# Attention loads: queries and keys sent without the pace of the other loads and ahead of value halves, a wider pace, weights a slot later

## The chip, the cores and the metric

The kernel runs on one core of one Trainium2 chip. The metric is the device time of one execution in microseconds, lower is better.

## The reference

An attention with global and local tokens is followed by two feed-forward layers. Batch is 4, there are 8 heads of 64, 512 local and 32 global tokens.

```python
k_all = np.concatenate([k_g, k_l], axis=2)
v_all = np.concatenate([v_g, v_l], axis=2)
out_g = np.matmul(sm(scale * np.matmul(q_g, k_all.transpose(0, 1, 3, 2))), v_all)
s_ll = scale * np.matmul(q_l, k_l.transpose(0, 1, 3, 2))
s_ll = np.where(np.abs(pos[:, None] - pos[None, :]) <= 32, s_ll, -1e9)
s_lg = scale * np.matmul(q_l, k_g.transpose(0, 1, 3, 2))
out_l = np.matmul(sm(np.concatenate([s_lg, s_ll], axis=-1)), v_all)
x = np.concatenate([out_g, out_l], axis=2)      # 4 x 8 x 544 x 64 -> 2176 x 512
h = x @ w_in                                    # 512 x 2048
x = np.where(h > 0, h, np.exp(np.minimum(h, 0)) - 1) @ w_out
h = x @ w2_in                                   # the second layer
x = np.where(h >= 1, h, np.where(h <= -1, 0, (h + 1) ** 2 / 4)) @ w2_out
```

## The kernel before, in words

The program has two stages. In the first, the planned stage, every instruction of every engine is pinned to the order in which it is written (`eng = pinned`; its records all carry line 113, the line of the helper `Pinned`). In the second (`eng = free`, from line 756 on) a scheduler orders the instructions of the two feed-forward layers.

The planned stage works through 24 units: for each batch and each two pairs of heads a local unit of the first pair, a global unit of both pairs, and a local unit of the second pair. Three units in turn, with two pairs of heads, are called a period here. A unit has parts (`scores`, `top`, `expo`, `turn`, `copy`, `values`, `norm`, `back`, `high`, `low`), and the loop over `n` at line 726 runs the scores of unit `n`, the values of unit `n - 1` and the end of unit `n - 2` in one slot, with pieces of the first layer's weights (`early_weights`) and of its first matmuls (`early_ups`) between. At the end of a slot `arrive(n)` issues loads. `r = n % 3` is the slot within a period: 0 for the slot of the first local unit, 1 for that of the global unit, 2 for that of the second local unit.

All loads of this stage go out on SyncE's queue, in order. They are:

- the queries `q_sb` (544 words of 4 bytes on each of 128 partitions) and the keys `k_sb` (576 words) of a pair of heads, by `load_qk`, two buffers each. The buffer of the keys comes free when the global unit's scores (`sg`) or the second local unit's (`s`) have read it. Before a pair's local scores GpSimd spreads its keys inside the buffer (`spread_keys`), and before the global scores it copies the global queries to `diag` (`spread_queries`);
- the values `v_sb` of a pair in two halves (1040 words each), by `load_v`, six buffers. `V_UNTIL` and the formula beside it in `arrive` say how many halves have been sent by the end of slot `n`;
- six pieces of the first layer's weights, `wraw` (1024 words each, one buffer): `next(next(sent, ...))` sends one at `r == 2`, that is in slots 2, 5, 8, 11, 14 and 17. `early_weights` takes the pieces up from slot 4 on, three slots for each: in slots 4, 7, 10 and so on ScalarE (`top`, line 180) and VectorE (`rest`, line 181) read the raw words for the first time, in the next slot VectorE for the last time.

`load` sets a pace: from the seventh load on, each load waits until the loads sent before it, counted back from itself, are landed as far as they don't fit into `IN_FLIGHT` words per partition together with it (2700 words are 1.38 MB). The wait is SyncE's, and all later loads stand behind it.

Order of the loads over one period, from slot `r = 2` on, before: (q k w v) (v v) (q k v). The brackets are slots.

Of the kernel before, what the change touches and what calls it, by code (L numbers as in the profile page):

```python
# [51 lines left out]

UP_STEP = 4

V_UNTIL = {0: 2, 1: 4, 2: 6, 3: 8, 4: 9, 5: 11}

LAG = 3

W_SHARE = 0.7

IN_FLIGHT = 2700
FIRST_LOADS = 6
WARM_UP = 10

# [2 lines left out]
def band_attention_then_two_mlps(  # L67
# [55 lines left out]

    loads = []

    def load(out, src, words):

        ins = eng.sync.dma_start(out, src)
        if eng is not pinned:
            return  # L130
        flying, older = words, len(loads)
        while older and flying + loads[older - 1][1] <= IN_FLIGHT:
            older -= 1
            flying += loads[older][1]
        if older and len(loads) >= FIRST_LOADS:
            tc.add_manual_dep(
                ins.ins, loads[older - 1][0].ins.name, LANDED, reason="loads in flight"
            )
        loads.append((ins, words))
# [22 lines left out]
    def prep(wraw_p, wtmp_p, layer, f, c0, n, raw_tag="wraw"):  # L162
# [7 lines left out]
        hi, lo = (w[:, c0:c0 + n] for w in wtiles[layer, f])  # L170
        raw = wraw_p.tile([P, n], U64, tag=raw_tag, name="wraw")
        load(raw, (w1, w2)[layer][f][:, c0:c0 + n], 2 * n)
        words = raw.bitcast(U32).rearrange("p (n two) -> p n two", two=2)
        low, high = words[:, :, 0], words[:, :, 1]
# [202 lines left out]
    with ExitStack() as actx:  # L377
# [30 lines left out]
        def load_qk(b, hp):  # L408
            q_sb = raw_p.tile([P, S], F32, tag="q", name="q_sb")
            k_sb = raw_p.tile([P, KPAD + NSUB * 64], F32, tag="k", name="k_sb")  # L410
            both = [(q_sb, qT), (k_sb[:, 0:KPAD], kT)]
            for sb, dram in both if b + hp else both[::-1]:
                load(sb, dram[b, hp], sb.shape[1])
            loaded[b, hp] = [q_sb, k_sb, diag[(NPAIR * b + hp) % 4]]

        def load_v(b, hp, es=(0, 1)):
            for e in es:
                v_sb = win_p.tile([P, half, 2, VW], F32, tag="v", name="v_sb", bufs=6)
                load(v_sb, vwin[b, hp, :, half * e:half * e + half], half * 2 * VW)
                landed.setdefault((b, hp), []).append(v_sb)  # L420

        def spread_keys(b, hp):

            k_sb = loaded[b, hp][1]
            right = k_sb[:, KPAD:].rearrange("p (a c) -> p a c", a=NSUB)
            after = k_sb[:, SG + 32:KPAD].rearrange("p (a c) -> p a c", a=NSUB)
            glob = k_sb[:, 0:SG].rearrange("p (o c) -> p o c", o=1)
            if b + hp == 0:
                eng.vector.tensor_copy(right[:, :, 0:32], after)
                eng.scalar.activation(  # L430
                    right[:, :, 32:64], glob.to_broadcast([P, NSUB, SG]), AF.Copy
                )
                return
            eng.gpsimd.tensor_scalar(right[:, :, 0:32], after, 1.0, 1.0, ALU.mult, ALU.mult)
            eng.gpsimd.tensor_scalar(
                right[:, :, 32:64], glob.to_broadcast([P, NSUB, SG]), 1.0, 1.0, ALU.mult, ALU.mult
            )

        def spread_queries(b, hp):

            for c in (hp - 1, hp):
                if hp % 2:
                    q_sb, dq = loaded[b, c][0], loaded[b, c][2]
                    for h in range(2):
                        r = 64 * h
                        eng.gpsimd.tensor_scalar(
                            dq[r:r + 64, 32 * h:32 * h + 32], q_sb[r:r + 64, 0:32], 1.0, 1.0,
                            ALU.mult, ALU.mult,
                        )
# [194 lines left out]
        pairs = [(b, hp) for b in range(B) for hp in range(NPAIR)]  # L644
# [8 lines left out]
        for _ in range(WARM_UP):  # L653
            eng.tensor.matmul(idle, zeros[:, 0:P], zeros)
        load_qk(*pairs[0])
        eng.scalar.dma_start(mask_sb, mask)
        eng.scalar.dma_start(eye_sb, eye)
        load_qk(*pairs[1])
        load_v(*pairs[0])
        for t in diag:  # L660
# [45 lines left out]
        def arrive(n):  # L706

            g, r = divmod(n, 3)
            p = 2 * g + 1
            if r == 1 and p + 1 < len(pairs):  # L710
                load_qk(*pairs[p + 1])
            elif r == 2 and p + 2 < len(pairs):
                load_qk(*pairs[p + 2])
                next(next(sent, iter([0])))
            while ahead and len(ahead) > 2 * len(pairs) - V_UNTIL.get(n, 4 * g + 5 + r):
                load_v(*ahead.pop(0))
            if r == 0 and g and p < len(pairs):
                spread_queries(*pairs[p])
            elif r == 1 and p < len(pairs):
                spread_keys(*pairs[p])  # L720
            elif r == 2 and p + 1 < len(pairs):
                spread_keys(*pairs[p + 1])

        ahead = [(*pair, (e,)) for pair in pairs[1:] for e in range(2)]
        live, first = {}, {}
        for n in range(len(units) + 2):
            if n > UP_AT:
                next(ups, None)
            part(n, "scores")
            part(n - 2, "norm")  # L730
            part(n - 1, "turn")
            part(n - 1, "copy")
            part(n - 2, "back")
            part(n - 2, "high")
            part(n, "top")
            part(n - 2, "low")
            part(n, "expo")
            if n >= PREP_AT:
                next(weights, None)
            if n >= UP_AT:  # L740
                next(ups, None)
            part(n - 1, "values")

            arrive(n)
            if n == len(units):

                s_ctx.close()
                ps_dn.append(mpool("ps_dn0", 1, space=PSUM))
                for f in chunks[0][1]:
                    down(0, chunks[0][1], 0, f, made[0, f, 0], first, range(KT // 2))  # L750
# [139 lines left out]
```

## Time and profile before

| | |
|---|---|
| median of 3 runs | 871.85 us (870.28 to 872.03) |
| profiled execution | 869.4 us, span of its instructions 867.6 us |
| granted TensorE clock, mean | 0.994 of full |
| matrix multiplies, busy | 847.8 us, 98% of the span |
| VectorE, ScalarE, GpSimd busy | 584.1, 431.6, 27.8 us |
| DMA | 65.43 MB, 75 GB/s over the span |

PE is TensorE's matrix multiply, PEld its weight load, DVE VectorE, ACT ScalarE, POOL GpSimd, SP SyncE, and a q behind an engine's name its queue (an instruction that is issued, not executed). Times of rows are counted from the start of the span. The time between an engine's instructions is called idle, and a releaser is what ended it as far as semaphores show. "issue" is time in which the engine waited for nothing that the profile shows. The planned stage ends near 138 us.

### The profile page before, as it was taken

How to read it: one execution, taken by the hardware profiler on the slowest of the kernel's cores; microseconds unless marked ns; L12 is line 12 of the kernel's file. 1: busy time of each engine (PE TensorE's matmuls, PEld its weight loads, DVE VectorE, ACT ScalarE, POOL GpSimd, SP SyncE). 2: the span in 40 equal slices, each digit the busy share in tenths (PEclk: the TensorE clock that was granted, in tenths of full speed). 3: DMA queues.
4: the chain of work that ended last, by engine and by line, in shares of the span. 5: the costliest groups of instructions: out<-in, count | busy, mean ns of one | idle time of the engine just before them, and what ended most of it. 6: DMA issues, size and time to landing. Idle time of an engine off the chain costs nothing.

```text
span 867.6 us, 14526 instructions
## 1 busy us (share of the span) xinstructions
PE 847.8 (98%) x5946; PEld 696.9 (80%) x5946; DVE 584.1 (67%) x1130; ACT 431.6 (50%) x755; POOL 27.8 (3%) x66
## 2 busy tenths in 40 slices
PE   8888999999999999999999999999999999999998
PEld 5666778888888888888888888888888888888886
DVE  4688884878536873834389897368859754845455
ACT  5666874666335543533257564456335333433332
POOL 2113110000000000000000000000000000000000
PEclk9899999999999999999999999999999999999999
DMA  7777742321200220100012112002201200000014
GB/s 261 246 241 256 231 148 87 108 99 65 81 1 7 94 94 1 59 39 1 1 49 97 49 50 97 0 9 98 89 1 49 97 1 1 0 1 1 2 59 147
DMA packets 19027, 65.43 MB, mean 75 GB/s; under 512 B 3984, under 2 KB 4240, under 8 KB 15248
## 3 DMA queue, kind: packets, MB, share of 16 engines
q1 hardware_dynamic: 18672, 64.23, 21.7%
q8 instruction: 47, 0.77, 0.4%
q10 hardware_dynamic: 288, 0.26, 0.1%
q14 instruction: 20, 0.16, 0.1%
HBM read 60.03 MB, written 4.46 MB: 74 GB/s over the span
## 4 chain that ended last, share of the span: by engine, by line
PE 91%; DMA 7%; POOL 1%; ACT 0%; issue 0%; SPq 0%; DVE 0%; POOLq 0%
PE dn L320 40%; PE up L247 39%; DMA k_sb<-in_kT 3%; DMA v_sb<-in_vwin 3%; PE up L244 3%; PE dn L337 3%; PE pt L113 1%; PE s L113 1%; PE up L113 1%; PE po L113 1%; DMA wraw<-in_w 1%; POOL k_sb L113 1%; PE sg L113 1%; PE dn L113 0%; PE tg L113 0%; PE up L273 0%
## 5 line engine op out<-in xcount | busy, mean ns | idle before, releaser
L320 PE MATMUL dn<-gh,wh 128*128 128x512 f32 x506 | 196.9, 389 | 0.0
L320 PE MATMUL dn<-gl,wh 128*128 128x512 f32 x506 | 196.8, 389 | 0.0
L320 PE MATMUL dn<-gh,wl 128*128 128x512 f32 x506 | 196.3, 390 | 0.0
L247 PE MATMUL up<-xh,wl 128*128 128x512 f32 x492 | 192.5, 391 | 0.0
L247 PE MATMUL up<-xh,wh 128*128 128x512 f32 x492 | 191.6, 389 | 0.0
L247 PE MATMUL up<-xl,wh 128*128 128x512 f32 x492 | 191.6, 389 | 0.0
L278 ACT ACTIVATE gh<-g 128x512 fp32r<-128x512 f32 x123 | 77.8, 632 | 119.2 <-DVE g L267 71.9
L297 DVE TENSOR_TENSOR acc<-dn,acc 128x512 f32<-128x512 f32 x128 | 84.9, 686 | 48.5 <-PE dn L320 48.4
L282 DVE TENSOR_TENSOR gl<-g,gh 128x512 fp32r<-128x512 f32 x123 | 84.7, 689 | 39.2 <-ACT gh L278 38.1
L320 PEld LDWEIGHTS dn<-gl,wh 128*128 128x128 f32 x506 | 95.0, 188 | 19.8
L320 PEld LDWEIGHTS dn<-gh,wh 128*128 128x128 f32 x506 | 95.0, 188 | 19.5
L320 PEld LDWEIGHTS dn<-gh,wl 128*128 128x128 f32 x506 | 95.0, 188 | 19.4
L247 PEld LDWEIGHTS up<-xh,wh 128*128 128x128 f32 x492 | 92.4, 188 | 19.3
L247 PEld LDWEIGHTS up<-xl,wh 128*128 128x128 f32 x492 | 92.4, 188 | 18.9
L247 PEld LDWEIGHTS up<-xh,wl 128*128 128x128 f32 x492 | 92.4, 188 | 18.7
L258 ACT ACTIVATE g<-up,half_sb 128x512 f32<-128x512 f32 (+1 forms) x69 | 47.0, 681 | 113.6 <-PE up L247 104.9
L266 DVE SCALAR_TENSOR_TENSOR g<-g 128x512 f32<-128x512 f32 (+1 forms) x69 | 47.0, 681 | 59.4 <-ACT g L258 59.3
L264 DVE SCALAR_TENSOR_TENSOR g<-up,g 128x512 f32<-128x512 f32 x64 | 43.5, 679 | 62.4 <-ACT g L255 62.3
L253 ACT ACTIVATE g<-up 128x512 f32<-128x512 f32 x64 | 37.8, 591 | 87.0 <-PE up L247 81.8
L267 DVE TENSOR_TENSOR g<-g,e 128x512 f32<-128x512 f32 (+1 forms) x69 | 47.0, 681 | 3.6
L180 ACT ACTIVATE top<-wraw 128x1024 f32<-128x1024 f32 x29 | 33.6, 1157 | 28.4 <-DMA wraw<-in_w 23.3
L255 ACT ACTIVATE g<-g,one_sb 128x512 f32<-128x512 f32 x64 | 45.9, 717 | 1.8
(112 smaller groups left out, 931.5 us busy)
## 6 DMA issues: line engine op xcount, KB each, us to landing
wraw<-in_w SPq DMA_DIRECT2D x29, 1024.0 KB, 4.8
v_sb<-in_vwin SPq DMA_DIRECT2D x32, 520.0 KB, 4.8
k_sb<-in_kT SPq DMA_DIRECT2D x16, 288.0 KB, 3.9
q_sb<-in_qT SPq DMA_DIRECT2D x16, 272.0 KB, 4.4
outT<-acc SPq DMA_DIRECT2D x16, 256.0 KB, 2.1
wraw<-in_w SPq DMA_DIRECT2D x6, 512.0 KB, 4.3
outT<-acc_rows SPq DMA_DIRECT2D x4, 64.0 KB, 2.2
mask_sb<-in_mask ACTq DMA_DIRECT2D x1, 192.0 KB, 3.5
```

The costliest lines, as they stand in the source:

```text
L113: return lambda *args, **kw: tc.keep_in_program_order(fn(*args, **kw))
L247: eng.tensor.matmul(self.ps, w, x, start=k == 0, stop=k == 3 * KT - 1)
L253: eng.scalar.activation(self.g, self.ps, AF.Exp)
L255: eng.scalar.activation(self.g, self.g, AF.Relu, bias=one_sb, scale=-1.0)
L258: eng.scalar.activation(self.g, self.ps, AF.Relu, bias=half_sb, scale=0.5)
L264: eng.vector.scalar_tensor_tensor(g, self.ps, 0.0, g, ALU.max, ALU.subtract)
L266: eng.vector.scalar_tensor_tensor(g, g, 1.0, g, ALU.min, ALU.mult)
L267: eng.vector.tensor_tensor(g, g, self.e, ALU.add)
L278: eng.scalar.activation(self.gh, self.g, AF.Copy)
L282: eng.vector.tensor_tensor(self.gl, self.g, self.gh.bitcast(F32), ALU.subtract)
L297: eng.vector.tensor_tensor(a, ps, a, ALU.add)
L320: eng.tensor.matmul(banks[d], w[:, d * P:(d + 1) * P], g, start=f == fs[0] and k == 0, stop=f == fs[-1] and k == 2,)
```

## The change

`load` gets a parameter `paced`; queries and keys are sent with `paced=False`, so that they wait for no other load (they still wait for their own buffers, and later loads still count them). `IN_FLIGHT` goes from 2700 to 3200 words (1.64 MB). A piece of weights is sent at `r == 0`, from the second period on, in place of `r == 2`: in slots 3, 6, 9 and so on. In the slots `r == 0` one half of values less is sent, and in the slots `r == 1` one more, behind the queries and keys of that slot. The order over a period becomes (q k v) (w v) (q k v v).

```diff
-V_UNTIL = {0: 2, 1: 4, 2: 6, 3: 8, 4: 9, 5: 11}
+V_UNTIL = {0: 2, 1: 4, 2: 6, 3: 7, 4: 9, 5: 11}
...
-IN_FLIGHT = 2700
+IN_FLIGHT = 3200
...
-    def load(out, src, words):
+    def load(out, src, words, paced=True):
...
-        if older and len(loads) >= FIRST_LOADS:
+        if paced and older and len(loads) >= FIRST_LOADS:
...
-                load(sb, dram[b, hp], sb.shape[1])
+                load(sb, dram[b, hp], sb.shape[1], paced=False)
...
                 load_qk(*pairs[p + 2])
+            elif r == 0 and g:
                 next(next(sent, iter([0])))
-            while ahead and len(ahead) > 2 * len(pairs) - V_UNTIL.get(n, 4 * g + 5 + r):
+            while ahead and len(ahead) > 2 * len(pairs) - V_UNTIL.get(n, 4 * g + (4, 6, 7)[r]):
                 load_v(*ahead.pop(0))
```

## Rows read from the trace of the kernel before

**Rows 1.** The page: TensorE's busy time; instruction queue (packets, MB, DMA share).

```profile
PE 847.8 (98%) x5946; PEld 696.9 (80%) x5946; DVE 584.1 (67%) x1130; ACT 431.6 (50%) x755; POOL 27.8 (3%) x66
...
q8 instruction: 47, 0.77, 0.4%
```

**Rows 2.** Stretches: length, PE, PEld, DVE, ACT, POOL busy, clock, DMA share, GB/s.

```profile
138.40:867.60 729.20, 725.51 (x3243) 602.01 (x3240) 484.89 (x692) 337.41 (x509) 0.00 (x0) 1.00 0.14 49
...
2.00:8.00 6.00, 4.48 (x74) 2.09 (x74) 2.04 (x14) 1.69 (x6) 1.25 (x5) 1.00 1.00 342
2.00:112.85 110.85, 96.93 (x2253) 75.11 (x2253) 82.60 (x367) 76.86 (x204) 23.58 (x54) 0.95 0.78 251
...
51.04:67.47 16.43, 14.32 (x339) 11.35 (x339) 13.99 (x57) 11.80 (x31) 4.25 (x9) 1.00 0.76 242
```

**Rows 3.** TensorE's waits, 24 to 138 us: in total, times, longest.

```profile
PE s L113 <- POOL k_sb L113: 7.0, 5, 2.1
PE s L113 <- issue: 1.9, 2, 1.8
PE po L113 <- DMA v_sb<-in_vwin: 1.3, 1, 1.3
PE pog L113 <- DMA v_sb<-in_vwin: 0.9, 1, 0.9
PE tg L113 <- DVE og L113: 0.3, 1, 0.3
```

**Rows 4.** The chain that ended last, one period: start, us, what.

```profile
56.90 3.60 DMA v_sb<-in_vwin
...
60.57 5.07 DMA k_sb<-in_kT
...
65.78 1.64 POOL k_sb L113 x2
```

**Rows 5.** SyncE's waits, 9 to 121 us: in total, times, longest.

```profile
SPq L113 <- DMA v_sb<-in_vwin: 42.2, 25, 3.3
```

**Rows 6.** The page's DMA issues: KB each, median us to landing.

```profile
v_sb<-in_vwin SPq DMA_DIRECT2D x32, 520.0 KB, 4.8
k_sb<-in_kT SPq DMA_DIRECT2D x16, 288.0 KB, 3.9
q_sb<-in_qT SPq DMA_DIRECT2D x16, 272.0 KB, 4.4
...
wraw<-in_w SPq DMA_DIRECT2D x6, 512.0 KB, 4.3
```

**Rows 7.** TensorE's timeline: start, us, instruction, idle before and releaser.

```profile
31.00 1.03 PE L113 MATMUL pog<-v_sb,pgT 64*64 64x130 f32 x10 [0.91 <-DMA v_sb<-in_vwin]
33.74 1.96 PE L113 MATMUL s<-k_sb,q_sb 64*32 64x128 f32 x64 [1.71 <-POOL k_sb L113]
...
55.60 1.22 PE L113 MATMUL sg<-k_sb,diag 128*64 128x272 f32 x12
...
67.47 1.16 PE L113 MATMUL s<-k_sb,q_sb 64*32 64x128 f32 x64 [2.08 <-POOL k_sb L113]
...
82.99 1.83 PE L113 MATMUL s<-k_sb,q_sb 64*32 64x128 f32 x64 [1.20 <-POOL k_sb L113]
```

**Rows 8.** SyncE's timeline: issues of one period.

```profile
52.34 0.33 SPq L113 DMA_DIRECT2D wraw<-in_w  x1
...
60.57 0.33 SPq L113 DMA_DIRECT2D k_sb<-in_kT  x1
```

**Rows 9.** Stretches as in rows 2, where the granted clock is low.

```profile
32.00:38.85 6.85, 5.14 (x114) 4.28 (x116) 2.86 (x21) 1.81 (x6) 3.21 (x8) 0.50 0.83 273
83.20:86.63 3.43, 3.43 (x72) 2.73 (x56) 3.16 (x21) 1.23 (x2) 2.18 (x6) 0.50 0.65 204
```

**Rows 10.** The weights' load of 52.34: flight; ScalarE's timeline: its first reader.

```profile
DMA to landing us min/median/max: 4.5/4.5/4.5
...
59.63 0.70 ACT L113 ACTIVATE top<-wraw 128x512 f32<-128x512 f32 x1
```

## The prediction

> **What bounds the kernel now.** I read the page first: TensorE is busy 847.8 of 867.6 us [rows 1], so at most 19.8 us of the span are to be had without removing matmuls. The windows by stage then say where these lie. From 138.4 us to the end, TensorE is busy 725.51 of 729.20 us [rows 2]; the edit touches only the planned stage before that, and a shift there moves the end by the same amount. Third, the waits of TensorE between 24 and 138 us [rows 3]: 7.0 us in five waits of the score matmuls `s` for the keys that GpSimd spreads, 1.3 and 0.9 us in one wait each for value halves, 1.9 us in the sequencer's own time ("issue"), 0.3 us for VectorE. Fourth, the chain that ended last, in one period of the stage (three units, two head pairs) [rows 4]: the end of the global scores is followed by a value half in flight for 3.60 us, then the keys in flight for 5.07 us, then GpSimd for 1.64 us, and only then the scores. The keys are not sent when their buffer is free but when a value half has landed. SyncE's own waits say the same in total: 42.2 us, 25 times, for value halves [rows 5]. The pace, not the buffers, orders this stage.
>
> The bytes of a period follow from the issues of the page [rows 6]: four value halves, two pairs of queries and keys, one piece of weights, 4 x 520 + 2 x 560 + 512 = 3712 KB, 3.80 MB. The stage moves 251 GB/s on the mean and 342 GB/s between 2 and 8 us, when the first loads are out together at a DMA share of 1.00 [rows 2]. At 251 a period takes 15.1 us, at 342 it takes 11.1. TensorE alone: from the end of `sg` (55.60 + 1.22 = 56.82) to the start of `s` at 67.47 are 10.65 us, 2.08 of them waiting [rows 7]; the window from `s` to `s` is 16.43 us long with 14.32 busy [rows 2]. So TensorE needs about 14.5 us, or 262 GB/s. Loads and TensorE are close, and a rate 5% above the present one makes TensorE the limit.
>
> **The change part by part.** *Queries and keys without the pace.* No instruction is added; two waits of SyncE per pair go. The keys' own buffer still makes them wait for the global scores. In the period shown the scores end at 56.82 and the keys go at 60.57 [rows 7, 8]: 3.75 us that the pace cost.
>
> *One value half goes behind instead of ahead.* The order on SyncE's queue was (q k w v)(v v)(q k v); it becomes (q k v)(w v)(q k v v). Counted along the queue, the period's first keys lose one 520 KB half ahead of them, 2.1 us at 251 GB/s or 1.6 at 342. The moved half now stands behind one query and one key load (560 KB, 2.3 us at 251); it is needed only a period later, so this costs nothing except at the start (below). With both parts the keys can go right behind the global scores, and must be spread 8.6 us later (10.65 less 2.08): 5.07 us in flight and 1.64 on GpSimd [rows 4] need 6.7. I take all four later waits as gone: 7.0 less the first, 1.71 [rows 7], is **5.3 us**. Bounds: 2.1 us for all of them together, if the loads stay the limit at 251 GB/s, since one half fewer ahead is then gained once and not per period; 5.3 at best.
>
> *The start.* The first three waits, 1.3 + 0.9 + 1.7 = 3.9 us, lie between 24 and 34 us. Two halves of values gain a 512 KB piece of weights that no longer stands ahead of them, so the 1.3 us goes. But the second half of the fourth pair now lands behind the fifth pair's queries and keys. Up to it there are 5 x 560 + 512 + 8 x 520 KB and 256 KB of constants, 7728 KB or 7.91 MB. From 2 us on that is 33.5 us at 251 GB/s, 25.1 at 342; at 280 it is 30.3. The value matmuls of the global rows would want it at 31.00 - 0.91 - 1.3 = 28.8 [rows 7]. At 280 they wait 1.5 us, and 2.4 of the 3.9 are won; the bounds are a loss of about 0.8 (matmuls end near 34.5 where `s` now starts at 33.74) and a gain of 3.9. I take **2.4**, with 280 as the rate, for the reason of the next paragraph.
>
> *3200 in place of 2700 words under way.* 18.5% more bytes in flight. If the rate went with them it would be 251 x 1.185 = 297 GB/s; half of that effect gives 274; the stretch without a pace shows 342. 280 is between, and above the 262 that TensorE needs. Bounds 251 and 342.
>
> *The clock.* In two stretches the granted clock is 0.50, the lower of its two levels (1.2 GHz): 6.85 us with 5.14 busy, and 3.43 us, all busy [rows 9]. The first begins as the wait of 1.71 us starts (33.74 - 1.71 = 32.03), the second 0.2 us after the wait that ends at 82.99 [rows 7]: both go with a wait for keys. The score matmuls take 1.96 us there and 1.16 elsewhere [rows 7], so 0.41 of the busy time is the price: 0.41 x 8.57 = 3.5 us. Fewer waits should take the second stretch (1.4) and, since a wait stays at the start, half of the first (1.05): **2.5**. Bounds 0 and 3.5.
>
> *What is late next.* Where no keys are waited for, the 0.3 us for VectorE shows [rows 3]; in the four periods freed I charge 0.3 each, **-1.2** (bounds 0 and, with VectorE busy 13.99 of 16.43 us [rows 2], some 2).
>
> *Code.* Two "issue" waits of together 1.9 us [rows 3] stand in the scores; with the value wait ahead of another run of scores gone, one more can show there: **-1.0**, bounds 0 and -1.8. The page has 47 instruction packets of 0.77 MB in all [rows 1], which more data under way could also delay. The Trainium skill (Runtime: NRT & Kernel Launch, section Instruction fetch mechanics) says that a sequencer fetches its next 16 KiB block through a DMA queue of its own while it executes, and that the cost is mostly hidden; the size agrees (0.77 MB / 47), the "issue" rows do not quite. By that page this term would be 0 and the sum 1.0 us better.
>
> *Weights a slot later.* A piece of weights went at 52.34, landed 4.5 us later at 56.84, and its first reader ran at 59.63 [rows 8, 10]: 2.8 us to spare. In the queue it now stands behind one more half, 2.1 us. It still fits, so I charge nothing; ScalarE, which would stand in `top` with the copies `pT` for TensorE queued behind it, is the cover that would be gone if it came later (rival 3). The wait of the weights for their own buffer (VectorE's reads) gets shorter by the slot.
>
> Sum: -5.3 - 2.4 - 2.5 + 1.2 + 1.0 = **-8.0 us**. The profiled execution took 869.4, so 861.4; the runs shown have a median 2.45 us above it (871.85), so I predict **863.9**.
>
> **The rivals.** *1. The wait only moves into the queue.* Keys sent earlier stand behind the same bytes, and the rate stays near 251. For it: the DMA share is already 0.78 over the stage [rows 2], and a landing takes 5.07 us for 288 KB, so loads do queue. Against it: the rate is 342 where nothing paces. It gives the one half, 2.1 us, and perhaps the 1.4 us of the second slow stretch less what the start loses (0.8): 869.7 down to 868, taken as 869. The Trainium skill (DMA: Bandwidth & Descriptors, section Queues, rings and completion order) has the rule behind this: SyncE's loads share one ring on each DMA engine, and descriptors are consumed in ring order, so an unpaced load does not overtake.
>
> *2. No change.* The keys might be held by their buffer and not by the pace, or a wait of VectorE or ScalarE takes the place of each one removed. For it: VectorE is busy 85% of the window. Against: the 3.75 us between the end of `sg` and the keys, and a value landing between the two in the chain. 871.85, within 0.2%.
>
> *3. Slower: the weights come late.* If the piece really goes a whole slot later, with the half of 4.6 us after it (56.90 [rows 4] less 52.34), and lands another 2.1 behind it, it is 6.7 us later, 3.9 past its reader; so five pieces with as little to spare cost at most 19.5 us, and nothing if the others have 6.7 to spare. Taken at 11, a little over the middle, less the 8.0 won, this is +3: 874.9. It decides from a cost of 1.9 us a piece on (8.0 + 1.7 over five), a delay of 4.7; one half is 2.1.
>
> **How the numbers follow.** 0.2% is 1.7 us, about what a measurement of this kernel can tell from no change. Forecast (gain of 5 to 12 us, 860 to 867): 0.60. Rival 1 (867 to 870): 0.22. Rival 2: 0.10. Rival 3: 0.08. The best case is 7.0 + 2.2 + 3.5 = 12.7 us with nothing given back, 859.1; I give less than 0.04 to anything under 860. The range 860 to 871 leaves out that, rival 3 and most of rival 2. Faster by over 0.2%: the forecast and nearly all of rival 1, 0.81; same 0.11; slower 0.08.
>
> **What would show it.** Right: the waits of `s` for GpSimd's keys fall from 7.0 to under 1.5 us; keys go within 1 us of the end of `sg`; periods of about 14.5 us; the stage's rate at 265 GB/s or more; matmuls of the free stage begin near 130 instead of 138.4; a wait of 1 to 2 us for values near 29 us. Rival 1: the keys' flight grows from 4 to 6 us or more, and they land when they did. Rival 3: ScalarE waits for `wraw` in `top`. The prediction is wrong if the rate does not rise above 262, if a value or weight wait larger than 2 us takes the place of the key waits, or if the clock falls in more places than two.

## The result and the profile after

The changed kernel takes 863.83 us (median of 4 runs, 860.65 to 864.34) against 871.94 us (870.28 to 874.63): ratio 0.9896, 95% interval 0.9862 to 0.9931, that is 6.0 to 12.0 us less. Its profiled execution took 864.34 us with a span of 862.6, so the two profiled executions are 5.1 us apart and the medians 8.1. The traces below account for the 5.1; the rest lies in the other runs, of which more further down.

Where the time went is read from the first matmul of the down products in TensorE's timeline, before and after (start, us, instruction):

```profile
134.03 0.50 PE L113 MATMUL dn<-gh,wl 128*128 128x512 f32 x1
```

```profile
128.95 0.50 PE L113 MATMUL dn<-gh,wl 128*128 128x512 f32 x1
```

From there to the end are 867.6 - 134.03 = 733.6 us before and 862.6 - 128.95 = 733.65 after. The whole difference lies in the planned stage, as forecast. TensorE's waits in that stage after the change, against [rows 3] (in total, times, longest):

```profile
PE po L113 <- issue: 2.6, 2, 1.8
PE s L113 <- issue: 1.8, 1, 1.8
PE tg L113 <- DVE og L113: 1.0, 3, 0.3
PE ot L113 <- DVE o_sb L113: 0.2, 1, 0.2
```

No wait for keys is left (7.0 us before) and none for values (2.2). What is left are waits of the sequencer's own, 4.4 us against 1.9, and VectorE's, 1.2 against 0.3. The periods of the stage and its rate, to be held against [rows 2] (length, PE, PEld, DVE, ACT, POOL busy, clock, DMA share, GB/s):

```profile
2.00:105.00 103.00, 94.47 (x2234) 73.03 (x2233) 79.45 (x363) 75.57 (x201) 25.29 (x58) 0.98 0.84 275
...
46.06:60.34 14.28, 14.25 (x341) 11.35 (x339) 12.02 (x55) 11.84 (x33) 3.90 (x8) 1.00 0.83 262
60.34:75.04 14.70, 14.34 (x341) 11.36 (x339) 13.09 (x56) 12.33 (x34) 3.60 (x9) 1.00 0.79 260
75.04:89.76 14.72, 14.35 (x340) 11.38 (x339) 13.10 (x56) 12.33 (x34) 3.69 (x9) 1.00 0.78 261
```

From one run of scores to the next a period is 14.3 to 14.7 us with 14.3 busy: TensorE is the limit, at some 260 GB/s. The DMA share does not tell this: it was 0.76 to 0.78 before as well [rows 2], when TensorE waited for loads. SyncE's waits, against the 42.2 us of [rows 5]:

```profile
SPq L113 <- PE s L113: 21.7, 7, 5.8
SPq L113 <- PE pt L113: 16.5, 9, 3.9
SPq L113 <- DMA v_sb<-in_vwin: 11.4, 12, 2.0
```

Loads are now held back mostly by TensorE, whose reads make the buffers free, and much less by loads under way: SyncE's waits for landings of all kinds come to 17.9 us in that stretch, 66.5 before. The period of [rows 8], in SyncE's timeline after:

```profile
47.45 0.33 SPq L113 DMA_DIRECT2D wraw<-in_w  x1
47.88 0.37 SPq L113 DMA_DIRECT2D v_sb<-in_vwin  x1
48.36 0.87 SPq L113 DMA_DIRECT2D q_sb<-in_qT  x1
51.81 0.33 SPq L113 DMA_DIRECT2D k_sb<-in_kT  x1
53.66 1.68 SPq L113 DMA_DIRECT2D v_sb<-in_vwin  x2
```

The global scores of that period run from 50.61 for 1.22 us, to 51.83: the keys go as they end, where they went 3.75 us later before.

TensorE's clock, however, was no better in this execution. The stretches at the lower level, against [rows 9] (same columns as the periods):

```profile
35.74:39.16 3.42, 3.42 (x21) 2.57 (x20) 2.15 (x6) 0.36 (x2) 0.00 (x0) 0.50 0.93 309
104.01:110.84 6.83, 6.83 (x98) 5.11 (x97) 4.84 (x23) 4.43 (x12) 2.07 (x4) 0.50 0.63 185
```

Together 10.25 us, as long as before (10.28), and all of it busy where before 8.57 was. Each starts within a microsecond after one of the sequencer's waits, which in the timeline are these (the third wait ends at 103.16):

```profile
25.42 0.43 PE L113 MATMUL po<-v_sb,pT 128*32 128x65 f32 x16 [0.89 <-issue]
35.60 0.34 PE L113 MATMUL po<-v_sb,pT 128*32 128x65 f32 x3 [1.76 <-issue]
103.16 0.42 PE L113 MATMUL s<-k_sb,q_sb 64*32 64x128 f32 x8 [1.81 <-issue]
```

### The profile page after: what moved, and what is told of

It is laid out like the page before. It is cut to its first block, busy times and chain, and to the rows that moved or that the text cites. A ratio compares the mean times of both kernels' runs of the same rounds, so it can differ in the third digit from the quotient of the medians.

```text
span 862.6 us, 14522 instructions
## 1 busy us (share of the span) xinstructions
PE 849.1 (98%) x5946; PEld 697.5 (81%) x5946; DVE 580.8 (67%) x1130; ACT 431.6 (50%) x755; POOL 27.6 (3%) x66
## 4 chain that ended last, share of the span: by engine, by line
PE 96%; DVE 2%; issue 1%; ACT 1%
PE dn L320 40%; PE up L247 39%; PE up L244 3%; PE dn L337 3%; PE po L113 2%; PE s L113 2%; PE up L113 2%; PE pt L113 2%; PE pog L113 1%; PE sg L113 1%; PE tg L113 1%; PE ot L113 1%; DVE top L113 1%; PE dn L113 1%; PE idle L113 0%
```

## The experiments

The theory: the keys, and at the start the values, arrive in time, whichever part of the change does it, and waits for code take a part back. Code waits are those that the views call "issue"; that they are waits for code is a guess until the run with the moved code. The rivals: the width alone carries the gain; waits of the sequencer belong to runs of short matmuls and not to code; the weights' new slot has a share of its own. Ratios are to the kernel before on the same chip.

| kernel | median us | ratio (95%) | waits for keys | for values | "issue" waits |
|---|---|---|---|---|---|
| changed | 863.83 | 0.9896 (0.9862 to 0.9931) | 0 | 0 | 4.4 |
| changed, again | 863.9 | 0.9907 (0.9885 to 0.9928) | 0 | 0 | 4.5 |
| no pace for q, k alone | 872.29 | 0.9995 (0.9978 to 1.0012) | 8.0 | 1.9 | 0.2 |
| 3200 words alone | 866.08 | 0.9916 (0.9889 to 0.9943) | 1.9 | 0.7 | 7.2 |
| order alone | 866.91 | 0.9936 (0.9914 to 0.9959) | 0 | 1.5 | 3.8 |
| all but the 3200 words | 866.66 | 0.9919 (0.9890 to 0.9949) | 1.4 | 2.2 | 2.6 |
| all but the missing pace | 864.02 | 0.9905 (0.9880 to 0.9931) | 0 | 0.2 | 3.0 |
| all but the weights' slot | 863.95 | 0.9902 (0.9880 to 0.9925) | 0 | 1.7 | 4.1 |

The waits are TensorE's between 24 and 138 us of one profiled execution each. The next paragraphs take the runs one by one.

**Queries and keys without the pace, alone.**

```diff
-                load(sb, dram[b, hp], sb.shape[1])
+                load(sb, dram[b, hp], sb.shape[1], paced=False)
```

> Only queries and keys without the pace; order, 2700 words and weights as before. If the gain comes from the keys arriving in time, by whichever part frees them: the keys go right behind the last value half instead of after the landing of the one before, about 2 us earlier a period; the waits of s for the spread keys fall from 7.0 to 2-4 us, the time to 867-869 us. If the width alone carries the gain (rival): within 1.7 us of before.

It measured 872.29 us, no change, and the key waits are 8.0 us. Theory and prediction were wrong on this part. SyncE's waits and two of its issues:

```profile
SPq L113 <- DMA v_sb<-in_vwin: 44.5, 19, 4.8
```

```profile
44.85 0.42 SPq L113 DMA_DIRECT2D k_sb<-in_kT  x1
...
59.26 0.33 SPq L113 DMA_DIRECT2D k_sb<-in_kT  x1
```

The keys of 60.57 [rows 8] go at 59.26, 1.3 us earlier, and are 5.4 us in flight instead of 5.07 [rows 4]: 0.9 us won. Those that went at 46.18 and were 3.0 us in flight go at 44.85 and need 5.9: they land 1.5 us later than before. The rate stays at 250 GB/s (2 to 112.85 us, 251 in [rows 2]), and the value halves ahead, still paced, take the wait over. This is the first rival of the prediction, confined to one part: the wait moved into the queue. The rule of the Trainium skill that the prediction cites for it (DMA: Bandwidth & Descriptors, section Queues, rings and completion order: descriptors of one ring are consumed in ring order) agrees with these flights.

**The pace of 3200 words, alone.**

```diff
-IN_FLIGHT = 2700
+IN_FLIGHT = 3200
```

> Only the pace of 3200 words; queries and keys paced, order and weights as before. If the keys' place behind the paced values is what held them: the key waits fall from 7.0 to 3-5 us and the time to 868-870 us. If the width alone carries the gain (rival): key waits under 1.5 us and 863-865 us. In both, code waits of TensorE (its 'issue' waits) grow from 3.1 us towards 5 if they depend on the data under way.

It measured 866.08 us, in neither range and nearer the rival's. One wait for keys of 1.9 us is left of five, the mean rate from 2 to 105 us is 270 GB/s (253 before), and TensorE's own "issue" waits are the largest of all kernels:

```profile
PE s L113 <- issue: 5.5, 4, 2.2
PE s L113 <- POOL k_sb L113: 1.9, 1, 1.9
PE up L113 <- issue: 1.6, 1, 1.6
PE po L113 <- issue: 1.6, 2, 1.3
```

These rows count from 0 us on: 8.7 us of "issue" against 3.1 before in the same stretch. In this execution (867.47 us, 1.9 less than the profiled one of before) the sequencer's waits took back 5.6 us, more than the 5.1 us that the keys gained; in the median run 6.9 us are won, so the other executions must have lost less to something, and no trace here shows to what.

**The order, alone.**

```diff
-V_UNTIL = {0: 2, 1: 4, 2: 6, 3: 8, 4: 9, 5: 11}
+V_UNTIL = {0: 2, 1: 4, 2: 6, 3: 7, 4: 9, 5: 11}
...
+            elif r == 0 and g:
                 next(next(sent, iter([0])))
-            while ahead and len(ahead) > 2 * len(pairs) - V_UNTIL.get(n, 4 * g + 5 + r):
+            while ahead and len(ahead) > 2 * len(pairs) - V_UNTIL.get(n, 4 * g + (4, 6, 7)[r]):
```

> Only the order (one value half behind the queries and keys, weights a slot later); everything paced at 2700 words. If the keys' place in the queue counts: key waits 2-4 us, 866-869 us. If the width alone carries the gain (rival): within 1.7 us of before. Had the later weights a cost of their own, ScalarE would wait for wraw in top by more than 1 us in total.

It measured 866.91 us, as the theory had it, and did better on the keys: no wait for them is left at the old pace of 2700 words. At the start a value wait of 1.5 us shows, in the matmuls `pog` near 29 us where the prediction had expected one:

```profile
PE pog L113 <- DMA v_sb<-in_vwin: 1.5, 1, 1.5
```

The later weights make ScalarE wait once, 0.6 us in `top`. The rate from 2 to 105 us is 263 GB/s, at the old 2700 words: the order alone lifts it from 253 to about what TensorE asks. So either of two parts brings most of the gain, and their gains don't add: 0.84% and 0.64% alone, about 1.0% together.

**All but the 3200 words.** The changed kernel with `IN_FLIGHT = 2700`.

> The whole change, but with the pace of 2700 words. If the keys' place and their missing pace carry the gain: key waits under 1.5 us and code waits of TensorE below the 5.6 us of the changed kernel, as less data is under way: 862-864.5 us, no slower than the changed kernel. If the width carries the gain (rival): key waits back at 4 us or more and 867-870 us.

It measured 866.66 us, between the two ranges: key waits are 1.4 us as the theory had it, but 2.2 us for values at the start, where the moved half stands behind queries and keys that nothing holds back. Beside the order alone (866.91) it shows again that the missing pace is worth nothing measurable.

**All but the weights' slot.** The changed kernel, the weights sent at `r == 2` as before.

```diff
                 load_qk(*pairs[p + 2])
-            elif r == 0 and g:
                 next(next(sent, iter([0])))
```

> The whole change, but each piece of weights goes out in its old slot, ahead of a value half. The sum charged the later slot at nothing: within 1.7 us of the changed kernel (862-865.5 us), no wait of ScalarE for wraw in either. If the later weights themselves bring part of the gain (rival: they stood ahead of the fifth and sixth value halves, and held SyncE until VectorE had read the piece before), the value wait near 25 us and key waits of 1 us or more come back, and the time is 865.5-868 us.

It measured 863.95 us, no difference, so the slot has no price and no gain that can be measured. The rival saw one thing rightly: the value waits at the start come back, 1.7 us.

**TensorE's code moved by 128 instructions.** The changed kernel, with another warm-up on zeros.

```diff
-        for _ in range(WARM_UP):
+        for _ in range(6):
             eng.tensor.matmul(idle, zeros[:, 0:P], zeros)
+        for i in range(68):
+            t = 32 * (i % 4)
+            eng.tensor.matmul(idle[t:t + 32, 0:64], zeros[:, 0:32], zeros[:, 0:64])
```

> The changed kernel with 128 instructions more in TensorE's warm-up: 6 of its 10 warm-up matmuls and 68 small ones of 64 columns, on zeros into the same unused tile, in about the same time. All later TensorE instructions stand 128 places further on. In the traces of before and after every 'issue' wait over 0.8 us stands at the same place modulo 256 instructions. If these are waits for code in blocks of 256 instructions: they leave the score and value runs where they stood and stand 128 program places earlier; these blocks hold fewer runs of short matmuls, so 1-4 us in total in place of 5.6, and the time falls by 1-4 us against the changed kernel (860-863 us). If the runs of short matmuls themselves make TensorE's sequencer wait (rival): the waits stay at the same instructions of the program, 5-6 us, 863.8.

It measured 862.86 us, ratio 0.9888 (0.9862 to 0.9914), with 4.1 us of "issue" waits from 0 us on, against 5.6 in the changed kernel. The waits moved to other instructions of the program. Counted between the ends of its waits (PE and PEld counts in brackets):

```profile
22.63:28.00 5.37, 4.03 (x124) 3.20 (x125) 3.35 (x8) 2.90 (x6) 0.73 (x2) 1.00 0.91 323
28.02:71.22 43.20, 41.35 (x1000) 32.39 (x1000) 37.76 (x164) 34.98 (x92) 12.66 (x27) 1.00 0.86 289
71.24:89.62 18.38, 16.88 (x376) 13.20 (x375) 15.88 (x74) 14.74 (x40) 3.84 (x8) 1.00 0.73 228
```

249, 2000 and 751 instructions are one, eight and three times 250. In the changed kernel the same counts, from 14.04 us on, are 499, 503 and 2998: two, two and twelve times 250.

```profile
14.05:25.41 11.36, 10.44 (x250) 8.33 (x249) 7.99 (x45) 9.73 (x28) 1.66 (x5) 1.00 0.85 263
25.43:35.58 10.15, 8.38 (x251) 6.60 (x252) 9.38 (x47) 7.54 (x24) 3.38 (x8) 1.00 0.96 328
35.61:103.15 67.54, 64.32 (x1499) 50.68 (x1499) 55.89 (x234) 52.37 (x134) 16.64 (x36) 0.97 0.81 267
```

With the few instructions of TensorE's queue that these columns leave out, that is 256 each. Counted in this way over all fourteen traces, each of the 41 "issue" waits of 0.4 us or more before 139 us stands at the same place modulo 256; only waits of 0.25 us and less stand elsewhere too. The rival is out: the long waits belong to the borders of blocks of 256 instructions, in every kernel run here.

The traces also show what ends them. The instruction queue q8 carries 47 packets of 16 KB in an execution [rows 1], and the end of each of the 41 waits comes 1.2 to 1.6 us after one of them has landed. At the 228 borders up to 140 us that TensorE passed without a wait, the block's packet had always landed at least 1.1 us before. For the wait of the changed kernel that ends at 35.60 us, the packet starts between 33.3 and 33.4 us (packets, MB, share of 16 engines in this tenth of a microsecond: 60.9% of 1.6 us, so it takes 0.97 us and lands near 34.3):

```profile
q8 instruction: 1, 0.02, 60.9%
```

So these are waits for code, and their length is how late the packet comes; what makes it late is not shown. The Trainium skill (Runtime: NRT & Kernel Launch, section Instruction fetch mechanics) gives 256 instructions for a block; the trace agrees. That the cost is mostly hidden holds in the free stage, where no such wait shows, but not here, where a block of short matmuls lasts some 5.6 us (67.54 us for twelve, above). The execution shown had no stretch at the lower clock and a span of 858.7 us.

**No pace at all.** The changed kernel with `IN_FLIGHT = 100000`.

> The changed kernel with no pace at all (loads wait for their buffers alone). If the code waits of TensorE grow with the data under way: more than 5.6 us, 7-10, key and value waits still under 1 us, 864-868 us. If they are set by the place in the program alone (rival): 5-6 us and 862.5-864.5 us.

It measured 864.84 us, ratio 0.9924 (0.9901 to 0.9947). Code waits came to 6.0 us, between the two expectations: not settled by the total. There are four. Three stand at places of the changed kernel, with other lengths (two of them below, the third 0.4 us near 106 us), and one of 1.25 us, near 61 us, at a border where the changed kernel had none:

```profile
26.29 0.43 PE L113 MATMUL po<-v_sb,pT 128*32 128x65 f32 x16 [1.55 <-issue]
37.28 0.30 PE L113 MATMUL po<-v_sb,pT 128*32 128x65 f32 x3 [2.83 <-issue]
```

**The changed kernel again,** beside the next three.

> The changed kernel once more, beside the three others on the same chip: 862-865.5 us, ratio 0.988-0.993. If a code wait of 1.5 us or more ends just before the granted clock falls in this trace too, the clock follows such waits; if the clock falls without one, it does not.

It measured 863.9 us. The same two places show once more, now with 1.81 and 2.72 us, and there is no wait near 103 us:

```profile
26.74 0.43 PE L113 MATMUL po<-v_sb,pT 128*32 128x65 f32 x16 [1.81 <-issue]
37.69 0.43 PE L113 MATMUL po<-v_sb,pT 128*32 128x65 f32 x3 [2.72 <-issue]
```

The place is fixed by the program; the length differs from one execution to the next, by 0.9 us and more (and the third wait was absent). The packets of code differ in the same way: for the wait near 37 us the packet landed at 34.33 us in the changed kernel, 36.42 in this execution and 35.80 with no pace, and the wait ended 1.3, 1.3 and 1.5 us later. The clock fell from 36.73 to 43.56 us, within the second wait (34.97 to 37.69), and not after the first.

**All but the missing pace.** The changed kernel with queries and keys paced.

```diff
-                load(sb, dram[b, hp], sb.shape[1], paced=False)
+                load(sb, dram[b, hp], sb.shape[1])
```

> The whole change with queries and keys paced as the other loads: the pace of 3200 words and the order alone. The missing pace alone gave nothing, and the change at 2700 words with or without it was the same. If the missing pace is worth nothing (theory now): 862-866 us, within 1.7 us of the changed kernel, key waits under 1 us. If it counts only where the rest is wide and in the new order (rival): key waits of 2 us or more and 866-868 us.

It measured 864.02 us, as the theory had it by then: the missing pace is worth nothing in the whole change either. This profiled execution (860.04 us) had code waits of at most 1.13 us, the clock at full throughout, and a span of 858.3, 4.3 us under that of the changed kernel's, its code waits 1.5 us shorter in all, and no other wait different by more than 0.4 us. Its matmuls are busy 845.5 us, 3.6 less than in the changed kernel (849.1) with its two stretches at the lower clock. That is what code waits and clock together can cost.

**The same with the code moved by 128.** The edits of the last run and of the moved code together.

> As the run before, with the 128 instructions more in TensorE's warm-up. If a block of code has its waits by its place, they leave the places of the run before; none over 1.5 us, the clock stays at full, 860-863.5 us. If the gain of the first kernel with moved code was chance or came from its shorter warm-up (rival): as the run before.

It measured 862.21 us, ratio 0.9879 (0.9854 to 0.9903), in the range named. But a wait of 3.20 us and a stretch at the lower clock from 28.78 to 39.02 us showed in the profiled execution, which the expectation excluded: moving the borders does not make the waits short.

```profile
29.43 1.01 PE L113 MATMUL s<-k_sb,q_sb 64*32 64x128 f32 x18 [3.20 <-issue]
```

**A short warm-up, code moved by 16.** As with 128, with `range(12)` in place of `range(68)`.

> The changed kernel with the warm-up of 6 matmuls and 12 small ones: as short a warm-up, but only 16 instructions more. The blocks then hold the runs of short matmuls much as before. If the place of the blocks counts: code waits of 5 us or more, one of them over 1.5 us with a fall of the clock behind it, 863-866 us. If the shorter warm-up brings the gain (rival): 860-863 us.

It measured 861.44 us, ratio 0.9881 (0.9862 to 0.9901). The expectation of 863 to 866 missed: code waits from 9 us on were 3.2 us, the longest 1.6, and the clock, low until 13.5 us (the first score matmuls took 1.96 us, as in [rows 7] at the lower level), stayed at full afterwards. That it rose so late cannot be put down to the shorter warm-up: in the next run, with the 6 matmuls alone, it rose at 3.9 us.

**A short warm-up alone.** The changed kernel with `WARM_UP = 6`.

> The changed kernel with 6 warm-up matmuls in place of 10, nothing added: blocks of code 8 instructions later in the program. If the shorter warm-up brought the 1 to 2.5 us of the kernels with moved code: 861-862.7 us. If the place of the blocks did: code waits at the old runs of the program, 5 us or more in total, 863-866 us.

It measured 862.15 us, ratio 0.9889 (0.9863 to 0.9915), in the range named for the shorter warm-up. Its profiled execution had 3.2 us of code waits, 2.98 of them in one, and three stretches at the lower clock. The four kernels with another warm-up lie 1.0 to 2.5 us under the changed kernel, but every interval overlaps with its own (0.9885 to 0.9928 on the same chip as two of them). Whether a shorter warm-up, the place of the borders or chance does that is open; none of them is shown to beat the changed kernel.

## Why the prediction was right, point by point

The sum was forecast as -8.0 us and measured as -8.1 in the medians. The terms were less good than the sum.

*The stage and the limit.* Right: all of it lies before the down products, TensorE became the limit, in periods of 14.3 to 14.7 us (forecast 14.5) at a rate of 275 GB/s from 2 to 105 us (forecast 265 or more).

*The keys, -5.3, and the start, -2.4.* All five key waits and both value waits went, 9.2 us of waits where these terms had 7.7. No wait of 1.5 us came at the start: the moved half of values went at 24.64 and landed 4.6 us later, at 29.3, when the value matmuls of the global rows had begun (28.24); no wait shows in them. By the working of that step that is 290 GB/s (7.91 MB from 2 us to 29.3), 10 above the rate taken.

*Why the keys came in time.* Here the prediction put the step wrongly. It had "the pace, not the buffers, orders this stage" and charged 3.75 us of delay to the pace of queries and keys. The pace of the values, and the order, were what counted: sent without a pace and nothing else changed, the keys gained nothing (872.29 us). One half fewer ahead (order alone, no key wait left) or more bytes under way (3200 words alone, one left) were each nearly enough. The bound of 2.1 us that the prediction set stood on the condition that the loads stay the limit at 251 GB/s, and the prediction had only the wider pace to lift that rate. The condition did not hold: with the order alone, at 2700 words, the rate is 263 GB/s and the gain 0.64%, 5.6 us.

*The clock, -2.5.* In the profiled execution nothing was won: 10.25 us at the lower level in place of 10.28, and all of it busy. The waits for keys that went with the falls were gone, but waits for code took that place. The price was set too high, too. In the execution with the clock at full throughout (all but the missing pace) matmuls are busy 845.5 us, so the slow stretches cost 2.3 us before (847.8), where the prediction had 3.5, and 3.6 after (849.1). Over the runs, however, the clock did gain. The profiled execution has the lowest mean granted clock of the changed kernel's ten runs (0.994 to 1.000, on the mean 0.997); 57 runs of the kernel before, beside the experiments, have 0.988 to 0.996, on the mean 0.993. With two levels that is, as an estimate, 4.5 us of an execution at the lower one in place of 12.4; at the two prices just named, 0.22 and 0.35 us for each of these (2.3 over 10.28 and 3.6 over 10.25), some 2 to 3 us are won. So the term was about right over the runs, though not in the execution shown, and its price was not.

*VectorE, +1.2.* 1.2 us against 0.3: +0.9. *Code, +1.0.* 4.4 against 1.9: +2.5, beyond the bound of 1.8. That a run of matmuls that no longer waits for its data shows a code wait was right, but the prediction looked for it in the scores and sized it by one; two of the three stand in value matmuls, at block borders, each as its packet came. *Weights, 0.* Right by the run with the old slot.

By the profiled pair: waits -7.0 - 2.2 and 0.4 at the very first scores (a query that now lands before them), +2.5 for code, +0.9 for VectorE make -6.2; matmuls are busy 1.3 us longer (849.1 against 847.8), the slow stretches; -4.9 against a span shorter by 5.0. The medians differ by 3.0 us more than these two traces. The clock of the other runs, some 2 to 3 us by the estimate above, would make up most of it; the rest is within the spread, as the kernel's own runs range over some 4 us and those of before over 4 to 7. That the forecast came within 0.1 us is luck: the waits for keys and values gave 1.5 us more than forecast and code took 1.5 us more, which cancels. That it lay between 5 and 12 is not.

## What to carry to other kernels

When a chain shows a load that waits for another load's landing, taking the wait from that load alone only lets it queue behind the same bytes; change what stands ahead of it, or how much may be under way, and expect either to be nearly enough. Once the loads are in time, look at what kept pace with them unseen: here the fetch of TensorE's own code, at every 256th instruction, in a stage of matmuls so short that a block lasts some 5.6 us. And a sum that comes out right is not yet a set of terms that are right: take it apart against the trace, one part of the change at a time.

## What the runs showed of the hardware

- TensorE's waits of 0.4 us or more without a releaser, 41 in the fourteen traces up to 139 us, all stand at borders of 256 instructions and end 1.2 to 1.6 us after a packet of the instruction queue has landed. The place is the program's: three executions have waits at the same two (26 and 37 us: 0.89 and 1.76, 1.81 and 2.72, 1.55 and 2.83 us). The length is the packet's lateness, and what sets that is open: with 2700 words under way the waits were 0.2 to 3.8 us in total after 24 us, with 3200 words 3.0 to 4.5 in the kernels of the table and 7.2 with 3200 words alone, with no pace 6.0, but TensorE was also less held by data in these.
- The clock fell in eleven of the fourteen traces after the warm-up, mostly within a microsecond of a wait of 1.2 us or more, but a wait of 2.1 us [rows 7] and others of 1.6 and 1.8 us had no fall behind them. A rule for which waits do it was not found.
